# Funnel attention and a gated feed-forward layer on one core: gate products split by tokens between two row tiles, four PSUM banks in one pool, the order from a plan

## Chip, cores and metric

One core of one Trainium2 chip. The metric is device time in microseconds, from the start to the end of one execution. All inputs and outputs are float32 in device memory; the kernel works in float16 with float32 accumulation.

## What is computed

The reference, cut to the core:

```python
# q, k, v: 8 batches x 8 heads x 1152 x 64
q_pool = q.reshape(B, H, S // 2, 2, D).mean(axis=3)          # 576 queries
attn = softmax(q_pool @ k.T / sqrt(D))                       # per head
x = (attn @ v).transpose(0, 2, 1, 3).reshape(B * 576, H * D) # 4608 tokens x 512
a = x @ w1                                                   # 512 x 1024
b = x @ w2
h = a * b @ w3                                               # 1024 x 1024
out = h @ w_out                                              # 1024 x 512
```

`a * b @ w3 @ w_out` is computed as `(a * b) @ T` with `T = w3 @ w_out`, formed once on the chip.

## The kernel before

**Attention.** Two heads of a batch make a pair P (0 to 31, four to a batch, named hp within it); u is the head in the pair. A pair's scores are 9 blocks of 128 keys by 576 queries; laid end to end over all pairs they are cut into 324 chunks of 512 columns. For each chunk c, `scores` issues matmuls of 64 rows, one head on each half of the TensorE array (partitions 0 to 63 and 64 to 127: two row tiles, which run side by side), into `psc` (two buffers of two banks). `expo` has ScalarE (ACT) write the exponentials to the ring `er`. When the chunks of a pair are done, `attend(P, u)` (a "burst") issues 45 matmuls of 128 rows into the bank `po`; column 64 of each block of 66 holds the row sum. VectorE (DVE) takes reciprocals (`rz`), multiplies (`xn`), and after the second head two DMA transposes on SyncE's queue (SP) write the pair's 576 tokens to `xT`, 128 rows of the model dimension by tokens.

**Preparation.** Pairs 0 to 8 have their keys and queries transposed by TensorE (`prep_pe_q`, then `prep_pe_k` in a later chunk, both through the bank `po`), the later ones by DMA transposes on SP (`prep_dma`). Loads run on GpSimd's (POOL's) queue.

**Feed-forward.** Nine units of 512 tokens. A gate block `pa` holds x·w1, `pb` x·w2, for one slice ft of 128 of the 1024 columns: 4 products of 128 rows. In the chunk loop each product is split by rows into two products of 64 rows on the two row tiles, both accumulating into the same bank. The second half trails the first by six products, and between them stands a copy of one element of the bank by VectorE, `handed`, which keeps the two row tiles out of one bank at the same time. `pa` is copied to `asb`, `pb` multiplied by it into `gT`. Then `rows` forms 128 tokens of output `pp` from 8 products with T, scaled into `osb` and stored by SP. Three banks (`spare`, tags ff0 to ff2) serve these blocks in turn. T itself is made of eight blocks `pT`, after `w3_transpose`.

**Order.** Each engine issues in the order in which the program is written out, which the chunk loop fixes by hand: scores and exp of the chunk, staging, then at most one of a burst, a preparation step or a w3 transpose, then at most one group of four products, if the summed cost `busy` lies below the due time `due`, which grows by PACE = 1.06 us a chunk. What is left after the loop is done with 128-row products: the rest of the parts, then `tail_ffn` for the last two units, where ACT does the `asb` and `osb` copies and the two-bank buffers of `psc` are used as well.

Of the kernel before, what the change touches and what calls it, by code (L numbers as in the profile page):

```python
# [23 lines left out]
def kernel(  # L24
# [21 lines left out]
    T_GRP, T_SC, T_PV, T_PREP, T_W3, PACE = 0.866, 0.219, 1.56, 0.7, 0.67, 1.06  # L46
# [9 lines left out]
    xT = const.tile([128, NC, NT], FP16)  # L56
    w1sb = const.tile([128, NC, dff], FP16)
    w2sb = const.tile([128, NC, dff], FP16)
    T16 = const.tile([128, NF, dm], FP16)
    wosb = const.tile([128, NF, dm], FP16)  # L60
    er = const.tile([128, 2, RING], FP16)
    vts = [const.tile([128, 2, NJ, VW], FP16, name=f"vt{i}") for i in range(4)]
# [13 lines left out]
    spare = [0, 1, 2]  # L76

    def bank(pre, dt=FP32, n=None):
        if n is None:
            n = spare.pop(0)  # L80
            spare.append(n)
        return psum.tile([128, 2048 // (4 if dt == FP32 else 2)], dt, tag=f"ff{n}", bufs=1,
                         name=pre)

# [81 lines left out]
    def prep_first():  # L166
# [6 lines left out]
        ta = bank("ta", FP16)  # L173
        tb = bank("tb", FP16)
# [30 lines left out]
    def prep_pe_q(P):  # L205
        pp, o = P // 2, 64 * (P % 2)
        new_kq(P)
        t2 = psum.tile([128, 1024], FP16, tag="po", bufs=1, name="t2")
        for c in range(NJ):
            nc.tensor.transpose(t2[:, 128 + 64 * c:192 + 64 * c],  # L210
                                qps[pp][o:o + 64, c].rearrange("p u d -> p (u d)"),
                                ident[o:o + 64, o:o + 64])
        keys(P, t2, range(8, 9))
        nc.vector.tensor_copy(out=qT[P].rearrange("p c f -> p (c f)"), in_=t2[:, 128:704])
        nc.vector.tensor_copy(out=kT[P][:, 8], in_=t2[:, 0:128])

    def prep_pe_k(P):
        t1 = psum.tile([128, 1024], FP16, tag="po", bufs=1, name="t1")
        keys(P, t1, range(0, 8))
        del kcs[P]  # L220
        nc.vector.tensor_copy(out=kT[P][:, 0:8].rearrange("p j f -> p (j f)"), in_=t1)

# [27 lines left out]
    def attend(P, u):  # L250

        po = psum.tile([128, 512], FP32, tag="po", bufs=1, name="po")
# [13 lines left out]
        if u == 0:  # L266
            xns[P] = ab.tile([128, 5, 2, D], FP16, tag="xn", bufs=3, name="xn")
        xn = xns[P]
        nc.vector.tensor_tensor(  # L269
            out=xn[:, :, u, :], in0=acc[:, :, 0:D],  # L270
            in1=rz.to_broadcast([128, 5, D]), op=ALU.mult)
        if u == 0:
            return
        b, hp = divmod(P, 4)
        n0 = b * SQ
        nc.sync.dma_start_transpose(
            out=xT[:, hp, n0:n0 + 512].rearrange("p (i r) -> p i r", r=128),
            in_=xn[:, 0:4].rearrange("p i u d -> p (i u d)"))
        nc.sync.dma_start_transpose(
            out=xT[:, hp, n0 + 512:n0 + SQ].rearrange("p (i r) -> p i r", r=64),  # L280
            in_=xn[64:128, 4].rearrange("p u d -> p (u d)"))
        del xns[P]
# [12 lines left out]
    def load_w(dst, src, cols=None):  # L295
        src = src.rearrange("(c p) f -> p c f", p=128)
        if cols is not None:
            dst, src = dst[:, :, cols], src[:, :, cols]
        nc.gpsimd.dma_start(out=dst, in_=src)

    def load_ffn(h):
        cols = slice(512 * h, 512 * h + 512)
        load_w(w1sb, moe_w1, cols)
        load_w(w2sb, moe_w2, cols)
# [3 lines left out]
    def w3_transpose(c):  # L308
        w3T[c] = ffp.tile([128, NF, 128], FP16, tag="w3T", bufs=4, name="w3T")
        t = bank("w3t", FP16)  # L310
# [4 lines left out]

    def T_half(c, o):
        if o == 0:
            pts[c] = bank("pT")
        for a in range(o, o + 4):
            nc.tensor.matmul(pts[c], w3T[c][:, a, :], wosb[:, a, :],  # L320
                             start=(a == 0), stop=(a == NF - 1))
        if o:
            nc.vector.tensor_copy(out=T16[:, c, :], in_=pts.pop(c))
            del w3T[c]

    pts = {}

    class Block:
# [4 lines left out]
        def __init__(self, pre, n_parts, then):  # L333
            self.pre, self.n_parts, self.then, self.n = pre, n_parts, then, None

        def product(self, part, n, h, lhsT, rhs):
            if self.n is None:
                self.n = spare.pop(0)
                self.t = bank(self.pre, n=self.n)
            s = slice(0, 128) if h is None else slice(64 * h, 64 * h + 64)  # L340
            last = h != 0 and part == self.n_parts - 1 and n == 3
            nc.tensor.matmul(self.t, lhsT(s), rhs(s), start=(h != 1 and part == 0 and n == 0),  # L342
                             stop=last, skip_group_check=True)
            if last:
                self.then(self.t)
                spare.append(self.n)
            elif n == 3:
                nc.vector.tensor_copy(out=handed, in_=self.t[0:1, 0:1])  # L348

    def parts_ffn(t):  # L350
        t0 = 512 * t
        held = {}

        def gate(ft, w, pre):
            def copy(t):
                held[ft] = ffp.tile([128, 512], FP32, tag="asb", name="asb")
                nc.vector.tensor_copy(out=held[ft], in_=t)  # L357

            def mul(t):
                if ft == 0:  # L360
                    held["g"] = ffp.tile([128, NF, 512], FP16, tag="g", name="gT")
                nc.vector.tensor_mul(out=held["g"][:, ft, :], in0=t, in1=held.pop(ft))  # L362
            block = Block(pre, 1, copy if pre == "pa" else mul)
            return [(block, 0, m, lambda s, m=m: w[s, m, ft * 128:ft * 128 + 128],
                     lambda s, m=m: xT[s, m, t0:t0 + 512]) for m in range(NC)]

        def rows(i):
            def store(t):
                osb = ffp.tile([128, dm], FP32, tag="osb", bufs=3, name="osb")
                nc.vector.tensor_scalar_mul(out=osb, in0=t, scalar1=1.0 / (SCL * SCL))  # L370
                store_rows(osb, t0 + 128 * i)
            block = Block("pp", 2, store)
            return [[(block, p, n, lambda s, ft=4 * p + n: held["g"][s, ft, 128 * i:128 * i + 128],
                      lambda s, ft=4 * p + n: T16[s, ft, :]) for n in range(4)] for p in (0, 1)]
        gates = [gate(ft, w, pre) for ft in range(NF) for w, pre in ((w1sb, "pa"), (w2sb, "pb"))]
        r = [rows(i) for i in range(4)]
        if held_back:
            gates.insert(2, held_back.pop())
        held_back.append(r[3][1])
        return gates + [r[0][0], r[1][0], r[2][0], r[0][1], r[1][1], r[2][1], r[3][0]]  # L380

    held_back = []
    parts, lag = [], []

    def product(x, h):
        x[0].product(x[1], x[2], h, x[3], x[4])

    def group():
        for x in parts.pop(0):
            product(x, 0)  # L390
            lag.append(x)
            if len(lag) > 6:
                product(lag.pop(0), 1)

    def store_rows(osb, r0):
        for s in range(2):
            b, f = divmod(r0 + 64 * s, SQ)
            rows = out[b * SQ:(b + 1) * SQ, :].rearrange("(p c) m -> c p m", c=NJ)
            nc.sync.dma_start(out=rows[f // 64], in_=osb[64 * s:64 * s + 64, :])

    def last_rows(pp, gT, r0):
        osb = ffp.tile([128, dm], FP32, tag="osb", bufs=3, name="osb")
        for h in range(2):
            hs = slice(256 * h, 256 * h + 256)
            if h == 1:
                pp = tail_bank("pp")
            for ft in range(NF):
                nc.tensor.matmul(pp[:, hs], gT[:, ft, 384:512], T16[:, ft, hs],
# [7 lines left out]
            for s in range(2):  # L416
                b, f = divmod(r0 + 64 * s, SQ)
                rows = out[b * SQ:(b + 1) * SQ, :].rearrange("(p c) m -> c p m", c=NJ)
                eng = nc.sync if s == 0 else nc.scalar
                eng.dma_start(out=rows[f // 64][:, hs], in_=osb[64 * s:64 * s + 64, hs])  # L420

    def tail_bank(pre, wide=False):
        if not wide:
            return bank(pre)
        return psum.tile([128, 2, 512], FP32, tag="psc", bufs=2, name=pre)[:, 0, :]

    def tail_ffn(t):
        t0 = 512 * t
        gT = ffp.tile([128, NF, 512], FP16, tag="g", name="gT")
        for ft in range(NF):  # L430
            pa = tail_bank("pa", ft % 2)
            for mc in range(NC):
                nc.tensor.matmul(pa, w1sb[:, mc, ft * 128:ft * 128 + 128],  # L433
                                 xT[:, mc, t0:t0 + 512],
                                 start=(mc == 0), stop=(mc == NC - 1))
            asb = ffp.tile([128, 512], FP32, tag="asb", name="asb")
            nc.scalar.copy(out=asb, in_=pa)  # L437
            pb = tail_bank("pb", ft % 2)
            for mc in range(NC):
                nc.tensor.matmul(pb, w2sb[:, mc, ft * 128:ft * 128 + 128],  # L440
                                 xT[:, mc, t0:t0 + 512],
# [108 lines left out]
    for x in lag:  # L550
        product(x, 1)
# [38 lines left out]
```

## Time and profile before

| | us |
|---|---|
| runs (3) | 461.23, 462.65, 464.69; median 462.65 |
| profiled execution | 460.9 |
| its span | 459.1 |
| TensorE clock granted | 1.0 throughout |
| first exp, last exp of the loop | about 8 and 400 |

The profile comes from one execution. PE is TensorE's matmuls, PEld its weight loads, DVE VectorE, ACT ScalarE, SP and POOL the queues of SyncE and GpSimd. In a group's line, the operation is followed by what it writes and reads with shapes, how often, the busy time in us and the mean ns of one, then the idle time of the engine ahead of it and what ended that. In a timeline the columns are start and duration in us, engine, line, operation, tiles, count, and in brackets the idle time and its releaser. A matmul's record includes its way through the array, so records overlap. Three windows, each of 20 us, with the engines' busy time:

| window (us) | PE | DVE | ACT | DMA engines' share |
|---|---|---|---|---|
| 40 to 60 | 18.29 | 10.23 | 15.94 | 1.20 |
| 200 to 220 | 18.27 | 12.29 | 15.85 | 1.01 |
| 420 to 440 | 20.00 | 4.98 | 7.01 | 0.23 |

### The profile page before, as it was taken

What the parts mean: (1) busy time and instruction counts of PE and PEld (TensorE: products, weight loads), DVE (VectorE), ACT (ScalarE), POOL (GpSimd) and SP (SyncE); (2) the same over time, 40 slices, a digit from 0 to 9 for tenths busy, and PEclk for the clock granted to TensorE, in tenths of its full rate; (3) what the DMA queues carried; (4) which work ended last, traced back from release to release, by engine and by line L of the source; (5) the groups of instructions that cost most, each with busy time, mean ns of one, the idle gap of its engine ahead of it and who ended that gap; (6) DMA issues with size and microseconds to landing.
All of it is one profiled execution on the core that took longest, in us unless ns stands there. A gap on an engine that the chain in (4) does not pass through costs nothing.

```text
span 459.1 us, 13873 instructions
## 1 busy us (share of the span) xinstructions
PE 421.1 (92%) x5834; PEld 247.1 (54%) x5834; DVE 235.9 (51%) x617; ACT 330.4 (72%) x351; POOL 81.1 (18%) x154
## 2 busy tenths in 40 slices
PE   3869999998899999998999999999999999999996
PEld 1535554554555556555555566555555555554443
DVE  2345554565556665565556556664666565543140
ACT  4768787887787888887788888887888888803332
POOL 8433321002030212122222222041022100000000
PEclk9999999999999999999999999999999999999999
DMA  8999999504889988898799979998998951012303
GB/s 129 206 208 198 200 190 164 88 14 57 127 133 197 153 130 130 166 166 114 117 171 174 138 109 140 159 144 122 171 173 136 131 121 39 15 37 68 70 23 91
DMA packets 94205, 58.78 MB, mean 128 GB/s; under 512 B 64832, under 2 KB 84544, under 8 KB 94144
## 3 DMA queue, kind: packets, MB, share of 16 engines
q0 software_dynamic: 26528, 33.56, 46.7%
q1 hardware_dynamic: 67456, 24.22, 32.3%
q8 instruction: 45, 0.74, 0.6%
q14 instruction: 16, 0.13, 0.1%
q10 hardware_dynamic: 160, 0.13, 0.1%
HBM read 67.11 MB, written 9.44 MB: 167 GB/s over the span
## 4 chain that ended last, share of the span: by engine, by line
PE 74%; ACT 10%; DVE 7%; DMA 4%; issue 2%; POOL 2%; ACTq 0%; SPq 0%; DVEq 0%; POOLq 0%
PE po L257 20%; PE psc L239 15%; ACT er L245 10%; PE pb L342 9%; PE pp L342 8%; PE pa L342 7%; DMA wosb<-in_moe_w_out_dram 4%; PE pT L320 3%; PE pb L440 3%; PE pa L433 3%; PE pp L450 2%; DVE handed L348 2%; PE t L163 1%; DVE xn L269 1%; DVE qp L122 1%
## 5 line engine op out<-in xcount | busy, mean ns | idle before, releaser
L245 ACT ACTIVATE er<-psc 128x1024 f16<-128x1024 f32 x324 | 314.2, 1027 | 79.6 <-PE psc L239 78.5
L239 PE MATMUL psc<-qT,kT 64*128 64x512 f16 (+7 forms) x1152 | 120.9, 290 | 7.5 <-ACT er L245 2.7
L342 PE MATMUL pb<-xT,w2sb 64*128 64x512 f16 x448 | 97.9, 376 | 5.6 <-DVE handed L348 3.0
L257 PEld LDWEIGHTS <-er 128*128 128x128 f16 x2880 | 91.7, 98 | 17.2 <-issue 16.3
L342 PE MATMUL pa<-xT,w1sb 64*128 64x512 f16 x448 | 97.9, 376 | 2.8 <-DVE handed L348 0.2
L257 PE MATMUL po<-vt,er 128*128 128x65 f16 x2880 | 99.4, 194 | 0.8 <-DVE xn L269 0.8
L239 PEld LDWEIGHTS <-kT 64*128 64x128 f16 x1152 | 53.0, 94 | 65.0 <-issue 30.0
L342 PE MATMUL pp<-T,gT 64*128 64x512 f16 (+1 forms) x416 | 73.7, 376 | 2.7 <-DVE handed L348 1.1
L362 DVE TENSOR_TENSOR gT<-pb,asb 128x512 f16<-128x512 f32 x56 | 38.7, 691 | 29.2 <-PE pb L342 29.0
L357 DVE COPY asb<-pa 128x512 f32<-128x512 f32 x56 | 38.7, 691 | 24.1 <-PE pa L342 23.7
L342 PEld LDWEIGHTS <-w2sb 64*128 64x128 f16 x448 | 33.7, 94 | 28.7 <-issue 12.1
L342 PEld LDWEIGHTS <-w1sb 64*128 64x128 f16 x448 | 33.7, 94 | 22.3 <-issue 6.0
L265 DVE RECIPROCAL rz<-po 128x5 f32<-128x5 f32 x64 | 12.4, 194 | 61.2 <-PE po L257 61.2
L342 PEld LDWEIGHTS <-gT 64*128 64x128 f16 (+1 forms) x416 | 27.0, 94 | 23.1 <-issue 6.2
L146 POOL COPY seen<-kT 1x1 f16<-1x1 f16 x21 | 3.7, 177 | 200.4 <-DMA kT<-kc 200.4
L269 DVE TENSOR_TENSOR xn<-po,rz 128x320 f16<-128x320 f32 x64 | 31.5, 491 | 2.4 <-DVE rz L265 0.3
L437 ACT COPY asb<-pa 128x512 f32<-128x512 f32 x16 | 9.4, 585 | 29.7 <-PE pa L433 29.7
L98 POOL DMA_DIRECT2D kst<-in_k_dram x33 | 23.7, 718 | 28.5 <-DVE kc L158 14.4
L370 DVE TENSOR_SCALAR osb<-pp 128x512 f32<-128x512 f32 x28 | 19.4, 692 | 14.4 <-PE pp L342 14.2
L105 POOL DMA_DIRECT2D vst<-in_v_dram x32 | 23.5, 733 | 12.8 <-DMA wosb<-in_moe_w_out_dram 4.7
L122 DVE TENSOR_TENSOR qp<-qst 64x1152 f16<-64x1152 f16 x31 | 23.2, 748 | 3.5 <-DMA qst<-in_q_dram 3.0
L443 DVE TENSOR_TENSOR gT<-pb,asb 128x512 f16<-128x512 f32 x16 | 11.1, 692 | 23.5 <-PE pb L440 23.5
(54 smaller groups left out, 237.2 us busy)
## 6 DMA issues: line engine op xcount, KB each, us to landing
qst<-in_q_dram POOLq DMA_DIRECT2D x32, 288.0 KB, 6.3
vst<-in_v_dram POOLq DMA_DIRECT2D x32, 288.0 KB, 7.8
out_dram<-osb SPq DMA_DIRECT2D x70, 128.0 KB, 2.8
kst<-in_k_dram POOLq DMA_DIRECT2D x31, 288.0 KB, 4.9
w3h<-in_moe_w_dram POOLq DMA_DIRECT2D x4, 512.0 KB, 15.5
wosb<-in_moe_w_out_dram POOLq DMA_DIRECT2D x1, 1024.0 KB, 16.7
xT<-xn SPq DMA_TRANSPOSE x64, 3.6
w1sb<-in_moe_w_dram POOLq DMA_DIRECT2D x2, 512.0 KB, 15.9
```

Of the source, the lines that this page charges most:

```text
L98: nc.gpsimd.dma_start(out=kst[P][:, :, js[0]:js[1], :], in_=k[b, h0:h0 + 2].rearrange("u (p j) d -> p u j d", j=NJ)[:, :, js[0]:js[1], :])
L105: nc.gpsimd.dma_start(out=vst[P].rearrange("p u j d -> p u (j d)"), in_=v[b, h0:h0 + 2].rearrange("u (p j) d -> p u (j d)", j=NJ))
L122: nc.vector.tensor_tensor(out=qps[pp][r].rearrange("p c u d -> p u c d"), in0=src[:, :, :, 0, :], in1=src[:, :, :, 1, :], op=ALU.add)
L239: nc.tensor.matmul(t[:, u, o:o + ln], kT[P][s, j, :], qv[s, f0:f0 + ln], start=True, stop=True)
L245: nc.scalar.activation(out=er[:, :, r:r + CH], in_=psc.pop(c), func=AF.Exp, bias=0.0, scale=SCALE)
L257: nc.tensor.matmul(po[:, VW * i:VW * i + D + 1], er[:, u, r:r + 128], vts[P % 4][:, u, j, 0:D + 1], start=(j == 0 and i == 0), stop=(j == ...
L269: nc.vector.tensor_tensor(out=xn[:, :, u, :], in0=acc[:, :, 0:D], in1=rz.to_broadcast([128, 5, D]), op=ALU.mult)
L320: nc.tensor.matmul(pts[c], w3T[c][:, a, :], wosb[:, a, :], start=(a == 0), stop=(a == NF - 1))
L342: nc.tensor.matmul(self.t, lhsT(s), rhs(s), start=(h != 1 and part == 0 and n == 0), stop=last, skip_group_check=True)
L357: nc.vector.tensor_copy(out=held[ft], in_=t)
L362: nc.vector.tensor_mul(out=held["g"][:, ft, :], in0=t, in1=held.pop(ft))
L370: nc.vector.tensor_scalar_mul(out=osb, in0=t, scalar1=1.0 / (SCL * SCL))
```

## The change

**Gate products.** `xn` is now per head, [128, 4, 64] with four buffers, and one DMA transpose of it puts a head's tokens on both halves of the partitions: blocks of 128 tokens alternate between the lower and the upper 64 partitions. The last 64 tokens of a batch go to `rems` and are transposed for two batches together into `xR`. The weights w1 and w2 stand on both halves too: loads by POOL to one half, then copies within SBUF to the other half, issued on SP's queue. So each row tile h works on its own tokens with all of the 512 rows, in 8 products of 64 rows. One block `pg` in one bank holds x·w1 in columns 0 to n-1 and x·w2 in columns n to 2n-1, 16 products in all; after the eighth, VectorE copies the first half of the bank to `asb` (`half`), after the sixteenth it multiplies the second half by it. n is 256 for the 512 main tokens of a batch (8 units), and 128 for the remaining tokens of four batches (2 units). No handover stands in a gate. T and output rows keep the split by rows and the handover.

**Banks.** `po` is no longer separate; four banks form one pool with times from the plan (`take`, `give`). Preparation takes two banks and transposes queries and keys in one go; each burst, w3 transpose and block takes one.

**Order.** The program models TensorE's time `pe`, VectorE's `vec` and the end of each exp, and `fill(until)` puts products from two streams, one for each row tile, until the exp before last is done; stream 0 leads stream 1 by up to LEAD. What is left is filled in after the loop.

```diff
-    T_GRP, T_SC, T_PV, T_PREP, T_W3, PACE = 0.866, 0.219, 1.56, 0.7, 0.67, 1.06
+    T_SC, T_PV, T_PREP, T_W3, T_EXP = 0.219, 1.57, 0.95, 0.7, 1.03
+    T_SEM, LEAD = 0.25, 2.3
...
-    xT = const.tile([128, NC, NT], FP16)
+    xT = const.tile([128, H, 2, 512], FP16)
+    xR = const.tile([128, H, 4, 64], FP16)
...
-    spare = [0, 1, 2]
+    spare = [(0.0, n) for n in range(4)]
...
     def load_ffn(h):
         cols = slice(512 * h, 512 * h + 512)
-        load_w(w1sb, moe_w1, cols)
-        load_w(w2sb, moe_w2, cols)
+        for dst, src in ((w1sb, moe_w1), (w2sb, moe_w2)):
+            src = src.rearrange("(c s p) f -> s p c f", p=64, s=2)
+            dst = dst.rearrange("p (c s) f -> s p c f", s=2)
+            for s in range(2):
+                nc.gpsimd.dma_start(out=dst[s, 64 * s:64 * s + 64, :, cols],
+                                    in_=src[s, :, :, cols])
+            for s in range(2):
+                nc.sync.dma_start(out=dst[s, 64 - 64 * s:128 - 64 * s, :, cols],
+                                  in_=dst[s, 64 * s:64 * s + 64, :, cols])
...
     class Block:
+        def ready(self, h):
+            if self.shared and h == 1:
+                return self.handed
+            if self.n is not None:
+                return 0.0
+            return spare[0][0] if len(spare) > keep else 1e9
...
+            if end and both and h == 0:
+                nc.vector.tensor_copy(out=handed, in_=self.t[0:1, 0:1])
+                self.handed = vector(1) + T_SEM
+            elif n == self.n_products // 2 - 1 and self.half:
+                self.half(self.t)
+            elif end:
+                give(self.n, self.then(self.t))
...
+        def gate(ft, h):
+            def copy(t):
+                a = g[h, ft] = ffp.tile([128, 256], FP32, tag="asb", bufs=4, name="asb")
+                if tail:
+                    nc.scalar.copy(out=a[:, 0:n], in_=t[:, 0:n])
+                else:
+                    nc.vector.tensor_copy(out=a[:, 0:n], in_=t[:, 0:n])
+                    vector(n)
+            def mul(t):
...
+                nc.vector.tensor_mul(out=g["t"][:, ft, h, 0:n], in0=t[:, n:2 * n],
+                                     in1=g.pop((h, ft))[:, 0:n])
...
+            block = Block("pg", 2 * H, False, mul)
+            block.half = copy
+            fs = slice(ft * 128, ft * 128 + 128)
+            for i, w in enumerate((w1sb, w2sb)):
+                for m in range(H):
+                    streams[h].append((block, H * i + m, slice(n * i, n * i + n),
+                                       lambda s, m=m, w=w: w[s, m, fs],
+                                       lambda s, m=m: x(s, m), ready))
...
+    def fill(until):
+        nonlocal pe, ahead, started
+        t = [pe, pe]
+        while True:
+            h = 0 if streams[0] and ahead < LEAD or not streams[1] else 1
+            if not streams[h]:
+                break
+            block, n, cols, lhsT, rhs, ready = streams[h][0]
+            cost = 0.003 + (cols.stop - cols.start) / 2400
+            if t[h] + cost / 2 > until:
+                break
+            at = max(ready[0], block.ready(h) if n == 0 else 0.0)
+            if at > t[h]:
+                if until < 1e8:
+                    break
+                t[h] = at
+            streams[h].pop(0)
+            t[h] += cost
+            ahead += cost if h == 0 else -cost
+            pe = max(t)
+            block.product(n, h, cols, lhsT, rhs)
+        pe = max(t)
...
-    early = [(10, 0), (11, 1), (19, 2), (20, 3), (28, 4), (30, 5), (32, 6), (34, 7)]
-    bursts = sorted([(last_chunk(P) + (1 if u == 0 else 5), P, u)
+    early = [(10, 0), (19, 2), (28, 4), (33, 6)]
+    bursts = sorted([(last_chunk(P) + (2 if u == 0 else 6), P, u)
                      for P in range(NP) for u in range(2)])
...
+        while ended and not early:
+            add_batch(*ended.pop(0))
+        keep = 2 if prepped < NPE and at + 0.3 >= due else 1 if bursts and bursts[0][0] <= c + 2 else 0
+        if c >= 1:
+            fill(exp_done[c - 1])
```

## The prediction

> **What bounds the kernel now.** I read the page first: busy shares, then the chain of waits, then the costliest groups.
>
> ```profile
> span 459.1 us, 13873 instructions
> PE 421.1 (92%) x5834; PEld 247.1 (54%) x5834; DVE 235.9 (51%) x617; ACT 330.4 (72%) x351; POOL 81.1 (18%) x154
> ...
> PE 74%; ACT 10%; DVE 7%; DMA 4%; issue 2%; POOL 2%; ACTq 0%; SPq 0%; DVEq 0%; POOLq 0%
> ...
> L342 PE MATMUL pb<-xT,w2sb 64*128 64x512 f16 x448 | 97.9, 376 | 5.6 <-DVE handed L348 3.0
> L257 PE MATMUL po<-vt,er 128*128 128x65 f16 x2880 | 99.4, 194 | 0.8 <-DVE xn L269 0.8
> ...
> L357 DVE COPY asb<-pa 128x512 f32<-128x512 f32 x56 | 38.7, 691 | 24.1 <-PE pa L342 23.7
> L269 DVE TENSOR_TENSOR xn<-po,rz 128x320 f16<-128x320 f32 x64 | 31.5, 491 | 2.4 <-DVE rz L265 0.3
> ```
>
> TensorE bounds it: 74% of the chain. But "busy" hides waits, because a matmul's record (376 ns) is longer than its streaming (the timeline steps by 216 ns at 512 columns, two 64-row products side by side). So I read the timeline next, in a stretch of the loop and at the loop's end.
>
> ```profile
> 398.13 0.69 DVE L362 TENSOR_TENSOR gT<-pb,asb 128x512 f16<-128x512 f32 x1 [0.65 <-PE pb L342]
> ...
> 398.35 0.40 PE L239 MATMUL psc<-qT,kT 64*128 64x448 f16 x4
> ...
> 398.74 0.13 DVE L348 COPY handed<-pb 1x1 f32<-1x1 f32 x1
> 398.88 0.39 PE L342 MATMUL pa<-xT,w1sb 64*128 64x512 f16 x2
> ```
>
> ```profile
> 411.36 1.24 PE L342 MATMUL pp<-T,gT 128*128 128x512 f16 x5
> ...
> 412.64 0.14 DVE L348 COPY handed<-pp 1x1 f32<-1x1 f32 x1 [0.17 <-PE pp L342]
> 412.84 1.02 PE L342 MATMUL pp<-T,gT 128*128 128x512 f16 x4 [0.23 <-DVE handed L348]
> ```
>
> In the first, TensorE restarts at the very end of the one-element copy (398.87). In the second, the fifth matmul starts at 411.36 + 4 x 0.216 = 412.22 and the next at 412.84: 0.62 us instead of 0.216, for a copy of 0.14. The round trip TensorE, VectorE, TensorE therefore costs 0.62 - 0.216 - 0.14 = 0.26 us beside streaming and the copy itself.
>
> Going through all matmul starts of the trace, I added up by how much each came later than the stream before it allowed, and by what had ended within 0.08 us before: 22 us end with a handed copy, 19 us with an exp (6 of them in the first 40 us), 9 us with an evacuation ahead of a key or query transpose. These are the sums the change can draw on.
>
> **The change, part by part.** The sum is made against the profiled execution: span 459.1, and 1.8 around it (460.9); the median of the runs is 1.75 above that.
>
> *Gate products.* Before, a gate is one block of 512 tokens and 64 rows twice, 4 products each: nine units of 16 blocks x 8 / 2 x 0.217 = 125 us (the last two with 4 full-height products a block, which costs the same). Now there are 8 units x 8 slices x 2 halves = 128 blocks of 16 products with 256 columns, and 2 x 8 x 2 = 32 blocks of 16 with 128. Score pieces give the pace of such pairs: two 256-column pairs in a row start 110 ns apart, two of 128 columns 56 ns. 2048 / 2 x 0.110 + 512 / 2 x 0.056 = 127 us: **+2**.
>
> *Weight loads* more than double (896 of 64 rows and 128 of 128 rows before, 2560 of 64 rows now). A probability-times-V burst loads 45 full weights in 1.54 us, 34 ns with its matmul; a pair needs two, 68 ns, which fits under 110 but not under 56: 256 pairs x 12 ns = **+3** (bounds 0 and 6). The Trainium skill speaks against the change here: TensorE: Matmul & The Clock Gate, section LDWEIGHTS, gives a load P / 1.2 ns, about 107 ns for 128 columns. By that, as an estimate, 2560 loads are 273 us, some 145 above the streaming; the burst row contradicts it and the measurement decides.
>
> *The handover of gates goes, a read in mid-block comes.* The 22 us of handed waits fall to about nothing (42 handovers stay, for T and output rows, with 2.3 us of lead): **-22**. But a gate's block now holds x·w1 in columns 0 to 255 and x·w2 in 256 to 511 of one bank. After the eighth product VectorE copies the first half; the ninth writes the other half of that bank. The plan sets no ready time for the ninth. Whether it waits for the copy no row shows, since every read and write ordered in the trace share bytes. Lower bound 0 (a read can't speed the ninth up). Upper bound from the 412.64 row, also a read in mid-block: 0.107 streaming + 0.26 + the copy, less the 0.110 normal step. The copy of 256 columns: the output copy at L414 has that shape, 424 ns. So 0.68; in the 64-row row (398.88) the restart is 0.05 sooner: 0.65 taken. For 128 columns the copy is 0.29 (691 ns at 512 and 424 at 256 give 1.04 ns a column on 158): 0.053 + 0.26 + 0.29 - 0.056 - 0.03 = 0.52. Between the two products stands one of the other half, in parallel, so it covers nothing. Queued behind the waiting ninth: all of TensorE's order, the scores that ACT waits for among it. 128 x 0.65 + 32 x 0.52 = 100 us. I take the wait as real: it is nearest to the row of a mid-block read of the same bank, and in the kernel before no engine reads a bank that is still to be written without such a wait. The Trainium skill (PSUM — Partial Sum Buffer, section PSUM bank collisions raise a hardware error) says that two engines on one bank and the same partitions raise an error "whether the two touch the same bytes or disjoint columns of the bank", so a kernel that runs must wait; no run here shows it, and the sum would be the same.
>
> Two corrections. The plan breaks into scores or a burst about 250 times over some 1330 pair slots; where a break falls just there (19% of 120 stalls in the loop) it covers 0.22, or all in one of four: -7. And the copy queues behind other VectorE work: per batch 8 bursts x 0.85, 4 preparations x 1.66, 4.5 outputs x 0.69, 17 us in some 62, each met with half its length (0.57 weighted): 0.155 x 160 = +25. Together **+118** (ends 0 and 160 x 0.9 = 144).
>
> *Order.* Scores are placed where the plan has the exp done; with TensorE slower than ACT, the 13 us of exp waits in the loop shrink to 2: **-11**. Preparation in two banks, queries and keys in one go, with its own banks instead of po: of 9 us, **-6**.
>
> *Normalising and transposes.* xn becomes two products (256 and 64 columns, 0.425 + 0.225 against 0.491); VectorE gains 10 us there and 34 in all, 270 of 460: hidden, it is no bound. SP issues 80 transposes instead of 64, some 1.25 us each: hidden, unless ahead of them something blocks, and it does:
>
> ```profile
> 35.66 0.77 POOL L299 DMA_DIRECT2D w1sb<-in_moe_w_dram  x1 [1.50 <-DMA w3h<-in_moe_w_dram]
> 38.25 0.74 POOL L299 DMA_DIRECT2D w2sb<-in_moe_w_dram  x1 [1.81 <-DMA kst<-in_k_dram]
> ...
> 47.00 0.74 POOL L299 DMA_DIRECT2D w2sb<-in_moe_w_dram  x1 [0.47 <-DMA qst<-in_q_dram]
> ```
> ```profile
> 31.11 1.32 SPq L276 DMA_TRANSPOSE xT<-xn  x1
> ```
>
> The eight new copies of weights to the other half of the partitions stand on SP's queue from chunks 4 and 14 on and wait for loads that land 16 to 17 us after these issues, at about 55 and 64. The first transposes, at 31 us before, now come behind them. xn has four buffers, one per head: the fifth burst (chunk 32, some 50 us) waits for the first transpose (about 60), the sixth for a transpose behind the second weights (about 70). VectorE stands behind xn, then the staging, then TensorE at the next preparation (near chunk 36). Their 2 MB also fall where the DMA engines are 80 to 90% busy. Bounds 0 and 15; **+8**.
>
> Sum: 459.1 + 2 + 3 - 22 + 118 - 11 - 6 + 8 = 551; with 1.8 around it, 553 for the profiled execution. The runs' median would lie 1 to 2 above; I say **553**.
>
> **The rivals.** (1) *Faster: no wait at the ninth product.* The same sum without 118 gives 435. It decides where writes to the second half of a bank go on while the first is read; break-even with before lies at a stall of (459 - 433) / 160 = 0.16 us per block, a quarter of the one priced. For it: the plan assumes it, and all other terms are gains. Against: the 412.64 row. Chance 0.09. (2) *The wait is there but mostly covered*, because the plan's breaks and late banks put other work between the halves: 0.3 x 160 = 48, so 483. Against: one stream's products follow each other directly unless a chunk ends. Chance 0.05. (3) *Weight loads bind too*: if the loads of a pair (94 ns each in the groups) did not overlap, 2560 x 0.094 = 241 us instead of 127, so 553 + 114 = 667. Against: 34 ns in the bursts. Chance 0.02. (4) *VectorE as bound*: 270 of 460 busy speaks against it; its queueing is in the 25.
>
> **How the numbers follow.** My forecast has 0.82; its own range takes the stall from 0.45 per block (72, with the other terms 507) to 0.9 and 15 for SP's queue (144 + 15, 586). The rest, 0.02, is near no change. The range of 495 to 595 holds nearly all of the forecast, leaving out the faster rival, the far slow one and most of (2). About 1% (4.6 us) is what a measurement tells from no change. Faster: 0.10, from (1) and a little of the rest; same 0.02; slower 0.88.
>
> **What the profile after would show.** Right, if the list of waits has TensorE's gate line waiting for VectorE's asb copy some 160 times; if the gate's ninth matmul starts at the end of that copy; if chunks in the gate stretches come every 1.6 us instead of 1.17 to 1.25; if ACT idles more and handed copies drop from 188 to 42. The SP step is right if xn waits for a transpose between 50 and 70 us. Wrong, if the ninth product starts while asb is being copied: then rival 1 holds. If exp starts come every 1.03 us and the tail is long, the plan did what it says. If gate pairs of 256 columns step by more than 110 ns without any wait, the loads bind.

## The result and the profile after

The changed kernel takes 574.9 us (median of four runs, 574.1 to 576.1) against 462.6 before: 1.242 times as long, 95% interval 1.237 to 1.248. The prediction was 553 us, 495 to 595, slower. Of each kernel's executions, those over 1.5% longer than its fastest are left out of the times below. The page of the profiled execution (575.3 us):

```profile
span 572.6 us, 17431 instructions
PE 443.3 (77%) x7514; PEld 326.3 (57%) x7514; DVE 246.8 (43%) x664; ACT 344.6 (60%) x398; POOL 82.2 (14%) x158
...
PEclk9999558999999999999999999999999999999997
...
L371 PE MATMUL pg<-xT,w2sb 64*128 64x256 f16 x1024 | 124.0, 269 | 58.5 <-DVE asb L409 42.2
...
L371 PE MATMUL pg<-xT,w1sb 64*128 64x256 f16 x1024 | 123.9, 270 | 0.0
```

The two gate lines are the result in small. The products with w1, which open a bank, never wait. Those with w2, which write the other half of the same bank, stand behind VectorE's copy. The share of TensorE's busy time fell from 92% to 77%, and ACT's from 72% to 60%: both wait. In the list of waits (who waited for whom; us in total, times, longest):

```profile
ACT er L263 <- PE psc L257: 129.0, 146, 27.8
...
PE pg L371 <- DVE asb L409: 51.4, 97, 1.6
...
DVE xn L287 <- DMA xT<-xn: 28.4, 2, 15.3
...
PE pg L371 <- ACT asb L407: 22.6, 57, 0.9
```

51.4 + 22.6 = 74 us in 154 waits, each for a semaphore of the reading engine, from which the list infers who ended it; before, TensorE's waits for asb were none and those for a handed copy 4.3 us by the same count. A matmul's record runs on after its streaming, so this count is low. By starts: each of the 160 asb copies is followed by a matmul that starts within 0.08 us of the copy's end, in 155 cases a gate product, and these 155 starts together come 99 us later than a step of 110 ns would have them. One of them, in the timeline:

```profile
302.35 0.27 PE L371 MATMUL pg<-xT,w1sb 64*128 64x256 f16 x1
...
302.45 0.38 PE L371 MATMUL pg<-xT,w1sb 64*128 64x256 f16 x2
...
302.56 0.38 PE L371 MATMUL pp<-T,gT 64*128 64x512 f16 x1
302.69 0.23 DVE L290 TENSOR_TENSOR rems<-po,rz 64x64 f16<-64x64 f32 x1
...
302.95 0.42 DVE L409 COPY asb<-pg 128x256 f32<-128x256 f32 x1
303.42 0.27 PE L371 MATMUL pg<-xT,w2sb 64*128 64x256 f16 x1 [0.48 <-DVE asb L409]
```

Eighth product, copy, ninth. The last product of x·w1 starts at 302.56, VectorE is still busy with the normalising of a burst, copies from 302.95 on, and nothing of TensorE's order starts until 303.42, though the ninth product writes columns 256 to 511 and the copy reads 0 to 255. The other stream's product (`pp`), which wants neither bank nor copy, stands behind it.

The second loss lies early. VectorE's timeline from 49 to 81 us, and SP's:

```profile
49.85 0.20 DVE L284 RECIPROCAL rz<-po 128x5 f32<-128x5 f32 x1 [2.30 <-PE po L276]
65.33 0.42 DVE L287 TENSOR_TENSOR xn<-po,rz 128x256 f16<-128x256 f32 x1 [15.28 <-DMA xT<-xn]
...
80.89 0.42 DVE L287 TENSOR_TENSOR xn<-po,rz 128x256 f16<-128x256 f32 x1 [13.08 <-DMA xT<-xn]
```
```profile
50.58 1.88 SPq L330 DMA_DIRECT2D w2sb<-w2sb  x2
52.50 2.06 SPq L298 DMA_TRANSPOSE xT<-xn  x1
61.21 2.59 SPq L330 DMA_DIRECT2D w1sb<-w1sb  x2
65.03 2.45 SPq L330 DMA_DIRECT2D w2sb<-w2sb  x2
67.58 40.31 SPq L298 DMA_TRANSPOSE xT<-xn  x9
```

The first transpose of xT is issued at 52.5 us (31.1 before), behind the first weight copies; those after the second weight copies only at 67.6. VectorE waits 15.3 and 13.1 us for a free xn buffer. Exp 36 (counted from 0) starts at 53.0 us and exp 40 at 85.1; before it was 55.1 and 59.6.

### The profile page after: what moved, and what is told of

Its sections match the earlier page's. It is cut to its first block, busy times and chain, and to the rows that moved or that the text cites. A ratio compares the mean times of both kernels' runs of the same rounds, so it can differ in the third digit from the quotient of the medians.

```text
span 572.6 us, 17431 instructions
## 1 busy us (share of the span) xinstructions
PE 443.3 (77%) x7514; PEld 326.3 (57%) x7514; DVE 246.8 (43%) x664; ACT 344.6 (60%) x398; POOL 82.2 (14%) x158
## 5 line engine op out<-in xcount | busy, mean ns | idle before, releaser
L371 PE MATMUL pg<-xT,w2sb 64*128 64x256 f16 x1024 | 124.0, 269 | 58.5 <-DVE asb L409 42.2
L371 PEld LDWEIGHTS <-w1sb 64*128 64x128 f16 x1280 | 93.2, 94 | 58.7 <-issue 52.4
L371 PEld LDWEIGHTS <-w2sb 64*128 64x128 f16 x1280 | 94.6, 94 | 53.4 <-issue 49.7
L371 PE MATMUL pg<-xT,w1sb 64*128 64x256 f16 x1024 | 123.9, 270 | 0.0
L415 DVE TENSOR_TENSOR gT<-pg,asb 128x256 f16<-128x256 f32 (+1 forms) x160 | 63.1, 397 | 98.5 <-PE pg L371 94.7
L276 PEld LDWEIGHTS <-er 128*128 128x128 f16 x2880 | 91.7, 98 | 15.3 <-issue 15.3
L371 PE MATMUL pp<-T,gT 64*128 64x512 f16 (+1 forms) x552 | 98.2, 380 | 0.0
L409 DVE COPY asb<-pg 128x256 f32<-128x256 f32 (+1 forms) x103 | 41.3, 401 | 29.1 <-PE pg L371 27.8
L287 DVE TENSOR_TENSOR xn<-po,rz 128x256 f16<-128x256 f32 x64 | 27.2, 425 | 30.7 <-DMA xT<-xn 28.4
L371 PE MATMUL pg<-xR,w2sb 64*128 64x128 f16 x256 | 21.8, 220 | 15.6 <-DVE asb L409 9.2
L371 PE MATMUL pT<-wosb,w3T 64*128 64x512 f16 x128 | 21.8, 397 | 2.7 <-DMA wosb<-in_moe_w_out_dram 2.7
```

The source lines that it names most:

```text
L276: nc.tensor.matmul(po[:, VW * i:VW * i + D + 1], er[:, u, r:r + 128], vts[P % 4][:, u, j, 0:D + 1], start=(j == 0 and i == 0), stop=(j == ...
L287: nc.vector.tensor_tensor(out=xn, in0=acc[:, 0:4, 0:D], in1=rz[:, 0:4].to_broadcast([128, 4, D]), op=ALU.mult)
L371: nc.tensor.matmul(self.t[:, cols], lhsT(s), rhs(s), start=(n == 0 and not (both and h == 1)), stop=(end and not (both and h == 0)), skip_ ...
L409: nc.vector.tensor_copy(out=a[:, 0:n], in_=t[:, 0:n])
L415: nc.vector.tensor_mul(out=g["t"][:, ft, h, 0:n], in0=t[:, n:2 * n], in1=g.pop((h, ft))[:, 0:n])
```

## The experiments

Theory A: the ninth product of a gate waits for the copy, since both touch one bank (in the program also one tile, the buffer named `pg`); with it goes a smaller loss by the place of the weight copies on SP's queue. Rival B: pairs of 256 and 128 columns are slow in themselves, by twice as many weight loads. Rival C: SP's queue is most of the loss. The first four runs stood side by side on one chip, where the kernel before took 463.1 us.

**Late copy.** The copy goes behind the sixteenth product:

```diff
             def mul(t):
+                copy(t)
                 if "t" not in g:
...
             block = Block("pg", 2 * H, False, mul)
-            block.half = copy
```

> The copy to asb moves from behind the eighth product to behind the sixteenth, so nothing reads a gate's bank while it is still to be written; the rest is the changed kernel. Theory A (the ninth product waits for the copy of the other half of its bank; in the profile of the changed kernel some 100 to 110 us of late matmul starts end with an asb copy): 575 - 105 = 470 us, 460 to 490, a bank being held 0.43 us longer; no matmul start waits for asb any more. Rival B (pairs of 256 and 128 columns are slow in themselves, by their doubled weight loads): 560 to 575. Rival C (SP's blocked queue early on is most of the loss): 565 to 580, since it is untouched here.

Measured: 476.7 us (473.8 to 480.2), 1.030 of before (1.023 to 1.037). 98 us are gone, with the copies and the loads as many as in the changed kernel. Rival B falls. In the trace 14 gate starts, 2 us in all, still end with a VectorE operation, and none with asb. Exp 40 stands at 85.2 us, in the changed kernel at 85.1, so the early loss is untouched, and rival C falls as the main cause.

**Weights by POOL.**

```diff
             for s in range(2):
-                nc.gpsimd.dma_start(out=dst[s, 64 * s:64 * s + 64, :, cols],
-                                    in_=src[s, :, :, cols])
-            for s in range(2):
-                nc.sync.dma_start(out=dst[s, 64 - 64 * s:128 - 64 * s, :, cols],
-                                  in_=dst[s, 64 * s:64 * s + 64, :, cols])
+                for o in (0, 64):
+                    nc.gpsimd.dma_start(out=dst[s, o:o + 64, :, cols],
+                                        in_=src[s, :, :, cols])
```

> Both halves of w1 and w2 are loaded from device memory by POOL instead of copied from half to half by SP; the rest, the mid-block copy included, is the changed kernel. Theory A with the SP step (chunks 36 to 40 took 32 us against 4.5 before, behind two waits of xn of 15.3 and 13.1 us): 575 - 28 = 547 us, 540 to 555, with exp 40 at about 57 us instead of 85. If the copies on SP's queue only shadow a DMA engine that is full anyway: 570 to 580, with exp 40 still near 80. If they are most of the loss (rival C): below 500.

Measured: 545.4 us (542.8 to 547.5), 1.177 of before (1.172 to 1.183); exp 40 at 58.4 us. The early loss is 29.5 us, and its cause lies among the eight copies on SP.

**Both.**

> Late copy and weights by POOL together. If the two losses are separate and add up: 575 - 105 - 28 = 442 us, 432 to 455, below the 462.6 of before. Rival B: about 545. If one loss hid behind the other: 455 to 475.

Measured: 451.3 us (447.9 to 453.3), 0.973 of before (0.967 to 0.980): the two losses add up within 4 us (98 + 29.5 against 123.6 together), and without them the change is faster than before, by 12 us and not by the 20 that I expected. The same two gate groups in this kernel's page:

```profile
span 449.5 us, 17294 instructions
PE 408.7 (91%) x7514; PEld 325.6 (72%) x7514; DVE 247.7 (55%) x664; ACT 336.1 (75%) x398; POOL 88.8 (20%) x166
...
PEclk9999999999999999999999999999999999999999
...
L369 PE MATMUL pg<-xT,w2sb 64*128 64x256 f16 x1024 | 117.2, 269 | 3.9 <-issue 3.9
L369 PE MATMUL pg<-xT,w1sb 64*128 64x256 f16 x1024 | 117.6, 269 | 0.0
```

As many products and weight loads as in the changed kernel, and no idle time ahead of the w2 products but 3.9 us of issue; in the list of waits TensorE no longer waits for asb.

**A read of one element in mid-block**, on top of both repairs:

```diff
+            def peek(t):
+                nc.vector.tensor_copy(out=handed, in_=t[0:1, 0:1])
+                vector(1)
             block = Block("pg", 2 * H, False, mul)
+            block.half = peek
```

> As with late copy and weights by POOL, and in addition VectorE reads one element of columns 0 to n-1 behind the eighth product; the ninth writes columns n to 2n-1, so the two share no byte. If the wait goes by bank: 160 x (0.107 + 0.26 + 0.14 - 0.16) = 56 us more than that kernel, with VectorE's queue up to 80: 495 to 525. If only shared bytes are ordered: the same as that kernel within 1%. It also gives the price of the bare round trip, beside the 256-column copy in the run with weights by POOL alone.

Measured: 545.3 us in the profiled execution; the other three took 554 to 557, so there is no interval. One element that shares no byte with the ninth product costs 94 us, as much as the copy of 256 columns (545.4). That the wait does not go by bytes is shown. Whether it goes by the bank or by the program's tile is not: the two are the same in every run here. The size I expected, 56 to 80, is missed. The trace says why: all 160 reads are followed by a matmul within 0.08 us of their end. Where VectorE was idle before the read (62 of them) TensorE lost 0.31 us in the median, less than the 0.35 expected. But 98 came to a busy VectorE, 67 of them behind a multiply, since copy and multiply now stand together at the end of the other stream's block, and those lost 0.74:

```profile
251.57 0.61 PE L369 MATMUL pg<-xT,w1sb 64*128 64x256 f16 x7
251.63 0.41 DVE L407 COPY asb<-pg 128x256 f32<-128x256 f32 x1
...
252.08 0.42 DVE L414 TENSOR_TENSOR gT<-pg,asb 128x256 f16<-128x256 f32 x1
252.42 0.13 DVE L420 COPY handed<-pg 1x1 f32<-1x1 f32 x1
...
252.61 0.27 PE L369 MATMUL pg<-xT,w2sb 64*128 64x256 f16 x1 [0.43 <-DVE handed L420]
```

In the changed kernel the split is the same in kind: 47 copies met an idle VectorE (0.58 us lost in the median), 56 a busy one (0.75), and 57 in the tail were ACT's.

**A bank each** for x·w1 and x·w2, with the copy where the changed kernel has it, behind the eighth product, and weights by POOL:

```diff
...
-                nc.vector.tensor_mul(out=g["t"][:, ft, h, 0:n], in0=t[:, n:2 * n],
+                nc.vector.tensor_mul(out=g["t"][:, ft, h, 0:n], in0=t[:, 0:n],
...
-            block = Block("pg", 2 * H, False, mul)
-            block.half = copy
             fs = slice(ft * 128, ft * 128 + 128)
-            for i, w in enumerate((w1sb, w2sb)):
+            for w, pre, then in ((w1sb, "pa", copy), (w2sb, "pb", mul)):
+                block = Block(pre, H, False, then)
                 for m in range(H):
-                    streams[h].append((block, H * i + m, slice(n * i, n * i + n),
+                    streams[h].append((block, m, slice(0, n),
```

> On top of weights by POOL: x w1 and x w2 of a gate get a bank each (two blocks of 8 products), and the copy stands at the same place as in the changed kernel, behind the eighth product. If the loss was the wait of the ninth product for its own bank (theory A), it goes here as with the late copy, though the copy still stands in the middle: 440 to 465 us, beside 452 with the late copy, and no late matmul start ends with asb. If the place of the copy in VectorE's queue is what costs, the time stays near 545.

Measured: 457.6 us (456.9 to 458.7), 0.987 of before (0.984 to 0.989; before 463.7 beside it). The same two groups in this kernel's page, now with a block each:

```profile
L369 PE MATMUL pa<-xT,w1sb 64*128 64x256 f16 x1024 | 117.9, 270 | 0.0
L369 PE MATMUL pb<-xT,w2sb 64*128 64x256 f16 x1024 | 117.7, 270 | 0.1
```

The copy in the same place no longer holds up the gate when the ninth product has another bank and tile; TensorE's waits for asb in the list are 2.8 us ahead of a `pp` and 0.9 ahead of a `po`, none in a gate. So it is the shared bank (or tile) and not the place.

**The plan's exp at 1.12 us**, with late copy and weights by POOL, and with a bank each.

```diff
-    T_SC, T_PV, T_PREP, T_W3, T_EXP = 0.219, 1.57, 0.95, 0.7, 1.03
+    T_SC, T_PV, T_PREP, T_W3, T_EXP = 0.219, 1.57, 0.95, 0.7, 1.12
```

> Late copy and weights by POOL, with the plan's time of an exp at 1.12 us instead of 1.03, so that more products stand between two chunks' scores. The prediction had the waits of scores for exp fall from 19 to 8 us; they rose to 23 and are 27 in the kernel with both repairs. If they come from scores that the plan places too early: they fall below 15 and the time to 440 to 448. If ACT is the bound by then: 455 to 465, and ACT idles more.

> A bank each for the two halves of a gate, weights by POOL, exp at 1.12 in the plan: the same change of the plan on the other repair. The difference to the kernel with a bank each should be that of the late-copy pair, -5 to -12 us, if scores placed too early are the cause in both; 440 to 455.

Measured: 449.0 us (two executions, 447.0 and 450.9) beside 451.3 (0.968 of before, 0.962 to 0.974, against 0.973, 0.967 to 0.980), and 457.9 beside 457.6 (0.989, 0.985 to 0.993, against 0.987). No gain clear of the intervals in either: the expected 5 to 12 us are missed, and my cause falls. The waits of scores for exp stayed at 25 us (27 with 1.03). They lie elsewhere than I had thought: 20 of the 27 us are in the first 100 us (14 of them between two chunks' scores, 4 ahead of T products), before any gate runs: the first gate product starts at 105.2 us there, before the change at 83.8. That TensorE has too little other work in that stretch, which no value in the plan can create, is argued from this and not tested.

**Weight copies on SP, but later**, with the late copy: the eight copies are issued at chunks 34 and 38.

```diff
+        if c in (34, 38):
+            spread_ffn((c - 34) // 4)
         scores(c)
         expo(c)
```

(`spread_ffn` holds the loop of copies taken out of `load_ffn`.)

> Late copy as before (478 us with the copies at their place), and the eight copies of w1 and w2 from half to half stay on SP's queue, but are issued at chunks 34 and 38 instead of 4 and 14, when their loads have landed or nearly so. If the place on SP's queue is what cost (they waited there for the loads, the xT transposes behind them, VectorE's xn behind those): 448 to 458 us, as with weights by POOL, and no wait of xn for a transpose over 3 us. If the 2 MB of copies cost by their traffic on the DMA engines, wherever they stand: 465 to 480.

Measured: 451.2 us (447.1 to 452.8), 0.974 of before (0.967 to 0.981). In the profiled execution (460.5 us) exp 40 stands at 58.7 us, and in SP's timeline the first five transposes now pass ahead of the copies:

```profile
24.48 27.94 SPq L298 DMA_TRANSPOSE xT<-xn  x5
52.47 1.98 SPq L335 DMA_DIRECT2D w1sb<-w1sb  x2
54.49 1.32 SPq L335 DMA_DIRECT2D w2sb<-w2sb  x2
55.90 1.24 SPq L298 DMA_TRANSPOSE xT<-xn  x1
62.46 2.73 SPq L335 DMA_DIRECT2D w1sb<-w1sb  x2
```

The traffic is the same, at nearly the same time (52 to 70 us, in the changed kernel 48 to 67), and the loss is gone: it was the place in the queue. The transposes issued between 50 and 75 us, most of them behind copies, took 14.8 us to landing in the median, in the changed kernel 12.2, and 6.9 with weights by POOL. So transposes behind the copies land late here too, but no `xn` waits for them any more.

## Why the prediction was right, and where its terms were not

The bound, the side and the mechanism held. **The wait in mid-block** was the largest term, +118 us. It measures 94 to 98 by the runs and 99 by the late starts. Two sizes in it were too large. The base of 0.65 per gate of 256 columns came out 0.58 in the median where VectorE was idle. And I put VectorE's queue on all 160 gates, while the 57 gates of the tail copy on ACT, where 51 met no queue (0.56 each in the mean, 99 - 24.1 - 43 = 32 us; 24.1 and 43 are the gates at an idle and a busy VectorE). The mean over all 160 is 0.62 (99 / 160) against 0.74 predicted. One sign of the prediction was off with it: chunks in the gate stretches came every 1.34 us (exps 100 to 320; 1.19 before) and not every 1.6. The rule from the Trainium skill, PSUM — Partial Sum Buffer, section PSUM bank collisions raise a hardware error, that two engines must be kept apart by bank and not by address, agrees with the one-element read; that a collision would raise an error was not tried. The prediction took from that section that a kernel that runs must wait; the section has such a kernel run to its end with an error and mostly wrong data, so it is a kernel with right results that must. The wait that the traces show is one that the program makes with a semaphore; what the chip would do without it, no run shows.

**Handover gone, -22**: held. No late start of a gate ends with a handed copy in the changed kernel but one of 0.1 us. For T the split by rows is new: its 64 products had 128 rows before and no handover, and are now 128 of 64 rows with 8 of the 42 handovers.

**Order, -11**: wrong in sign. Late starts behind an exp rose from 19 to 23 us, and to 27 with both repairs. I had put the waits down to scores placed too early in the loop; with both repairs 20 of the 27 us lie in the first 100 us, before the first gate. Why the changed order leaves more of them there stays open.

**Preparation, -6**: held where SP doesn't interfere; with weights by POOL the late starts ahead of transposes that end with a VectorE operation fall from 9 to 3 us.

**SP's queue, +8**: the chain was right link by link (weights landing, transposes behind the copies, the fifth and sixth burst's xn, the preparation near chunk 36), the size was not: 29.5 us, outside its bounds of 0 to 15. The prediction had the two waits end at about 60 and 70 us; they ended at 65.3 and 80.9, each 13 us after the issue of the transpose (52.5 and 67.6). The weights landed about when predicted (the two loads by 51.9 and 66.9, forecast about 55 and 64). What was missed is the transposes' own time: each was issued right behind four copies, 1 MB, and landed late, as the three medians above show (12.2 and 14.8 us behind copies on SP's queue, 6.9 without). How the copies delay them is not shown.

**Gate products and weight loads, +2 and +3**: the +2 held, the +3 is nothing. In the trace with both repairs a gate product starts 109 ns (median) after the last but one ahead of it at 256 columns, and 56 ns at 128: the paces taken from the score pieces, with nothing added for the loads, where the prediction let a pair at 128 columns take 68. Without the two waits, the streaming that remains after all late starts is 378 us (449.5 - 71) as before (459.1 - 81). The Trainium skill's load of about 107 ns for 128 columns (TensorE: Matmul & The Clock Gate, section LDWEIGHTS) does not bind here. With 2560 loads of 64 rows for the gates the repaired kernel is faster than before.

The sum erred to the low side, 553 against 575, as the too large wait (some 20 us) partly paid for the too small SP term (21) and the missed gains of the order (15 in the changed kernel); about 5 us stay open. That 553 came so near 575 is in part luck, since these errors have opposite signs. Rival 1, the sum without the wait, was 435, and without the +8 for SP's queue 427; with both losses repaired the kernel takes 451. Of the 24 us between, 19 are the order's term, -11 expected and +8 found; the rest stays open.

## What to carry to other kernels

Ask of every read of a PSUM bank whether a matmul into that bank is still to come, in whatever columns: if the program orders the two, as here, it costs a round trip through the reading engine's queue, here 0.3 us for one element with VectorE idle and 0.7 with VectorE at work, and all of TensorE's order stands behind it. A plan of an order must hold such waits as ready times, or it orders for a machine that isn't there. A DMA that waits for another DMA belongs on a queue, or at a place in it, where nothing urgent stands behind it.

## What the runs showed that I had not expected

TensorE stood idle from 55 to 81 us but for 1 us at 67, and its granted clock fell to half (the slices marked 5 in the row PEclk of the changed kernel's page: 40 slices of the span, in tenths of full clock); the repaired kernel's row has 9 throughout. The clock was still at half from 81 to 89 us, when the work had come back. Eight products for T, before the stretch and in it:

```profile
46.22 1.04 PE L371 MATMUL pT<-wosb,w3T 64*128 64x512 f16 x8
...
84.76 1.94 PE L371 MATMUL pT<-wosb,w3T 64*128 64x512 f16 x8
```

Beside the kernel with weights by POOL, the changed one is 26.7 us late at exp 40 and 29.0 at exp 42, so some 2 of the 29.5 us of the early loss fall into this slow restart. The Trainium skill, TensorE: Matmul & The Clock Gate, Part 1, says that an idle window of about 3.4 us returns the clock to half rate, and the row agrees in the rate; the window's length isn't read from a run here. And reads of one element were as dear in all as copies of 256 columns, 545.3 against 545.4 us. With VectorE idle they cost half as much (0.31 against 0.58 us), but 98 of 160 met a busy VectorE, where the queue is paid (0.74 and 0.75); of the copies only 56 did.
